# Attention, a gated layer and a merged layer in one kernel: output products ahead of the last pass, three buffers of split weights, a later input split, and a planner that ranks by PSUM tile

## The chip, the cores and the metric

The kernel runs on one core of one Trainium2 chip. The metric is the device time of one execution in microseconds (us); less is better. Five engines work side by side, each through its own queue of instructions in order: TensorE (PE, with its weight loads PEld), VectorE (DVE), ScalarE (ACT), GpSimd (POOL), and SyncE (SP), which here issues nearly all DMAs.

## The reference

```python
# attention: batch 4, 8 heads, 576 tokens, head_dim 64
scores = scale * np.matmul(q, k.transpose(0, 1, 3, 2))
thresh = np.max(scores, axis=-1, keepdims=True) - tau
scores = np.where(scores >= thresh, scores, -1000000000.0)
scores = scores - np.max(scores, axis=-1, keepdims=True)
attn = np.exp(scores)
attn = attn / (np.sum(attn, axis=-1, keepdims=True) + 1e-09)
attn_out = np.matmul(attn, v)
...
x = attn_out.transpose(0, 2, 1, 3).reshape(2304, 512)
# first layer, 512 -> 1536 -> 512
gate = 1.0 / (1.0 + np.exp(-(x @ w_gate)))
x = gate * (x @ w_val) @ w_out
# second layer, 512 -> 1024 -> 1024 -> 512
return ((x @ w1) * (x @ w2) @ w3) @ w_out2
```

All inputs are fp32, some handed over as float64 and cast on the core.

## The kernel before, in words

Every large product is made of three: each fp32 operand is split into a high part (an ACT copy, line 822) and a low part (a subtraction, line 823, on POOL or DVE), and the function `three` multiplies high by low, low by high and high by high into one PSUM tile. All matmuls carry line 439, that of the helper `mm`.

The program has two halves. In the first, a loop over 144 score blocks (`g`) does the attention: scores `ps_s` on PE, their maximum on DVE (`e`, line 687), two ACT passes over the exponentials (lines 695, 696), a split into two 16-bit halves (`h`, lines 703 and 707), a DMA transpose (`pt`) and the products with the values (`u`). Beside it runs a generator as filler: first `merge_gen`, which multiplies w3 by w_out2 into merged weights kept in DRAM as `sc_m`, then `l1_gen`, the first layer. That layer has four passes over the tokens, three of 512 columns and a last one of two halves of 384. A pass takes 12 units of `ps_h` products (`h_unit`: gate weights `gh`, `gl`, value weights `vh`, `vl`, input `xh`, `xl`), and after each three units an output stage `o_stage`: 4 tiles of `ps_o`, 9 products each. A stage stands in the list `pend` and is issued one unit later. The input of a pass is split by `xsplit(b)`, once the attention of that batch is finished; the last pass waits for all of it. `XR` is the buffer that holds attention output, then the layer's output.

What is issued up to the end of the attention is ordered by the class `Plan`: it builds the dependences, places the instructions forward in time by a table of costs (`order`), then backward (`backward`), and gives each instruction a rank by its backward start; the next forward placing prefers low ranks. Of `ROUNDS` such placings it pins the one whose PE ends first. Kinds of product on PE are told apart by a letter: W are 128-row split products (`ps_h`, `ps_o`).

The second half, after the attention, is ordered by the framework's scheduler from the order of the program. It finishes the last pass, then takes the tokens in three groups of 768. Per group, `x2split` makes seven pairs of input parts `o0h`, `o0l` to `o6h`, `o6l`; `pair` makes 8 feature blocks of products `ps_ab` with weight tiles `wc` (ten buffers, loaded by SP) and splits their results into `abh`, `abl`. Then comes the y stage: `part(i, t)` multiplies block `i` by the merged weights `wm(i)` for six row tiles `t`, 18 products of `ps_y` per `i`. `wm_load(i)` loads `wms` from `sc_m` and splits it:

```python
        for i in range(NF2 - 2):
            for t in range(GT // P):
                part(i, t)
            wms.append(wm_load(i + 2))
```

Of the kernel before, what the change touches and what calls it, by code (L numbers as in the profile page):

```python
# [9 lines left out]
F32R = mybir.dt.float32r  # L10
# [11 lines left out]
class Plan:  # L22
# [12 lines left out]
    STAY = 0  # L35
    NEAR = ("HH", "RH", "TH", "HT", "RT", "TT")
    TURN = {"HW": 86, "RW": 199, "WR": 90, "HR": 90, "TR": 90, "RH": 100, "RT": 145, "TW": 5, "HT": 34}
    ROUNDS = 6

    def __init__(self, insts, cut, over, beads=()):  # L40
        self.later = [i for i in insts[cut:] if i.opcode in self.OPS]
# [280 lines left out]
    def backward(self):  # L322
        N, E = len(self.x), ("PE", "DVE", "ACT", "POOL", "SP")
        pred = [self.hard[n] | self.soft[n] for n in range(N)]
        out = [0] * N
        for n in range(N):
            for q in pred[n]:
                out[q] += 1
        lat = [d - s for s, d in zip(self.start, self.done)]
        held = [  # L330
            c[0] if e in ("PE", "SP") else max(60, c[0] - self.OVER[e])
            for c, e in zip(self.cost, self.e)
        ]
        ready, begin = [0.0] * N, [0.0] * N
        avail = {e: [n for n in range(N) if not out[n] and self.e[n] == e] for e in E}
        free = dict.fromkeys(E, 0.0)
        for _ in range(N):
            best = None
            for e in E:
                if not avail[e]:  # L340
                    continue
                n = min(avail[e], key=lambda n: (
                    max(ready[n] + lat[n] - held[n] - free[e] - 1, 0), -self.done[n]
                ))
                s = max(free[e], ready[n] + lat[n] - held[n])
                if best is None or s < best[0]:
                    best = s, e, n
            s, e, n = best
            avail[e].remove(n)
            begin[n] = free[e] = s + held[n]  # L350
            for q in pred[n]:
                out[q] -= 1
                if q not in self.hard[n]:
                    r = begin[n] - lat[q]
                elif self.e[q] == self.e[n] != "SP":
                    r = begin[n] - (lat[q] - 5 if e == "PE" else 0)
                else:
                    r = begin[n] + self.LAG[self.e[q]] + self.LEAD[e]
                ready[q] = max(ready[q], r)
                if not out[q]:  # L360
                    avail[self.e[q]].append(q)
        for i, n in enumerate(sorted(range(N), key=lambda n: -begin[n])):
            self.rank[n] = i

    def pin(self, tc):
        best = None
        for i in range(self.ROUNDS):
            seq = self.order()
            end = max(t for t, e in zip(self.done, self.e) if e == "PE")
            if best is None or end < best[0]:  # L370
                best = end, seq, self.start
            if i + 1 < self.ROUNDS:
                self.backward()
        end, seq, self.start = best
        for n in seq["DVE"]:
            if self.cost[n][1]:
                for m in seq["POOL"]:
                    if self.start[m] > self.start[n]:
                        tc.add_manual_dep(
                            self.x[m], self.x[n].name,  # L380
                            mybir.DependencyInfo(mybir.DependencyClass.Sync, mybir.DependencyReason.DATA),
                            reason="port",
                        )
                        break
        for l in seq.values():
            self.turns(tc, [self.x[n] for n in l])
# [12 lines left out]
def kernel(  # L399
# [23 lines left out]
    P = 128  # L423
    B, H, S, D = q.shape
    NPAIR = H // 2
    NT, DM = out.shape
# [3 lines left out]
    NF = DFF // P  # L430
# [403 lines left out]
    def flush(keep):  # L834
        while len(defer) > keep:
            defer.pop(0)()
# [96 lines left out]
    def open_lx():  # L933
        nonlocal lx
        lx = lx_ctx.enter_context(tc.tile_pool(name="lx", bufs=1))

    def l1_gen():
        w32, whl, gv, pend, raws = {}, {}, {}, [], {}
# [63 lines left out]
        def xsplit(b):  # L1002
            o, k, w = passes[b]
            xh, xl = (lx.tile([P, KC, k * w], F32R, tag=z, name=z) for z in ("xh", "xl"))
            for j in range(k):
                js = slice(j * w, (j + 1) * w)
                for c in range(KC):
                    split(
                        xh[:, c, js], xl[:, c, js], XA[:, c, o + j * w:o + (j + 1) * w],
                        nc.vector if c % 2 else nc.gpsimd,  # L1010
                    )
            return xh, xl
# [80 lines left out]
        for F in range(NFT):  # L1093
            b, f = divmod(F, NF)
            if f == 0:
                while not ready(b):
                    yield None
                if b == B - 1:
                    lx_ctx.close()
                    open_lx()  # L1100
                xhl = xsplit(b)
            k, w = passes[b][1:]
            gv[F] = [
                tuple(
                    (lx if j else lb).tile([P, w], F32R, tag=g, name=g, bufs=4)
                    for g in ("gvh", "gvl")
                )
                for j in range(k)
            ]
            for j in range(k):  # L1110
                yield from h_unit(F, xhl, j)
            whl.pop(("g", F)), whl.pop(("v", F))
            if pend:
                yield from o_stage(*pend.pop())
            if f % SG == SG - 1:
                pend.append((b, f // SG))
                if F == NFT - 1:
                    flush(0)
                    yield from o_stage(*pend.pop())
                    flush(0)  # L1120
# [3 lines left out]
    def ready(b):  # L1124
        return xdone[0] > b and (b < B - 1 or tail[0])
# [145 lines left out]
    NG = NT // GT  # L1271
# [59 lines left out]
    def x2split(g):  # L1331

        t = {m: xp.tile([P, KH, HT], F32, tag="x" + m, name="x" + m) for m in ("1", "2")}
        ops = [
            tuple(xp.tile([P, KH, HT], F32R, tag=f"o{m}{z}", name=f"o{m}{z}") for z in "hl")
            for m in range(7)
        ]
        k1, k2 = slice(0, KH), slice(KH, KC)

        def put(m, x):  # L1340
            split(ops[m][0], ops[m][1], x)

        l, r = (XA[:, :, g * GT + h * HT:g * GT + (h + 1) * HT] for h in range(2))
        put(0, l[:, k1])
        nc.vector.tensor_tensor(t["1"], r[:, k1], l[:, k1], op=ALU.subtract)
        put(1, l[:, k2])
        put(2, t["1"])
        nc.vector.tensor_tensor(t["2"], r[:, k2], t["1"], op=ALU.subtract)
        put(3, t["2"])
        put(4, r[:, k2])  # L1350
        nc.gpsimd.tensor_tensor(t["1"], r[:, k2], r[:, k1], op=ALU.subtract)
        put(5, t["1"])
        nc.gpsimd.tensor_tensor(t["1"], l[:, k2], t["2"], op=ALU.subtract)
        put(6, t["1"])
        return ops

    wg_ = w12_gen()
    x2 = None
    while x2 is None or l1 is not None:
        l1 = run(l1, 4200.0)  # L1360
        if next(wg_, "end") == "end" and x2 is None:
            wctx.close()
            xp = ctx.enter_context(tc.tile_pool(name="xp", bufs=1, side="right"))
            x2 = x2split(0)
# [3 lines left out]
    sp = ctx.enter_context(tc.tile_pool(name="sp", bufs=1))  # L1368
# [90 lines left out]
            at, c0, left = at + m, c0 + m, left - m  # L1459

    def wm_load(i):
        t = sp.tile([P, 2, DM], F32R, tag="wm", name="wm", bufs=2)
        x = sp.tile([P, DM], F32, tag="y", name="wms", bufs=4)
        nc.sync.dma_start(x, sc_m[i])
        split(t[:, 0], t[:, 1], x, nc.gpsimd if i % 2 else nc.vector)
        return t
# [3 lines left out]
    for g in range(NG):  # L1470
        abs_ = [
            tuple(sp.tile([P, GT], F32R, tag=f"ab{z}{f}", name=f"ab{z}{f}") for z in "hl")
            for f in range(NF2)
        ]
        for i in range(NPR):
            if i == NPR - 1:
                wms = [wm_load(0), wm_load(1)]
            pair(x2, i, abs_)
        if g + 1 < NG:
            x2 = x2split(g + 1)  # L1480
        pss = [bank("ps_y") for _ in range(GT // P)]
        def part(i, t):
            h, l = abs_[i]
            ts_ = slice(t * P, (t + 1) * P)
            three(
                pss[t], (h[:, ts_], l[:, ts_]), (wms[i][:, 0], wms[i][:, 1]), i == 0, i == NF2 - 1
            )

        for i in range(NF2 - 2):
            for t in range(GT // P):  # L1490
                part(i, t)
            wms.append(wm_load(i + 2))
        end = len(nc.cur_bb.bb.instructions)
        for t in range(GT // P):
            part(NF2 - 2, t)
            part(NF2 - 1, t)
            out_rows(g, t, pss[t])
# [36 lines left out]
```

## Time and profile before

| what | us |
|---|---|
| median of 3 runs (1042.97 to 1045.5) | 1044.69 |
| profiled execution, its own time | 1041.44 |
| its span, first to last instruction | 1039.5 |
| PE busy / DVE / ACT / POOL | 985.5 / 616.7 / 652.9 / 699.3 |

The profile is of one execution. Its span leaves out 1.9 us around the first and the last instruction. Starts of rows are counted from the span's start. Matmuls are pipelined: a row's length is from issue to the modelled end, so the distance of two starts tells what a product costs PE, not its length.

### The profile page before, as it was taken

How to read it: one execution, taken by the hardware profiler on the slowest of the kernel's cores; microseconds unless marked ns; L12 is line 12 of the kernel's file. 1: busy time of each engine (PE TensorE's matmuls, PEld its weight loads, DVE VectorE, ACT ScalarE, POOL GpSimd, SP SyncE). 2: the span in 40 equal slices, each digit the busy share in tenths (PEclk: the TensorE clock that was granted, in tenths of full speed). 3: DMA queues.
4: the chain of work that ended last, by engine and by line, in shares of the span. 5: the costliest groups of instructions: out<-in, count | busy, mean ns of one | idle time of the engine just before them, and what ended most of it. 6: DMA issues, size and time to landing. Idle time of an engine off the chain costs nothing.

```text
span 1039.5 us, 20101 instructions
## 1 busy us (share of the span) xinstructions
PE 985.5 (95%) x7152; PEld 834.5 (80%) x7152; DVE 616.7 (59%) x1158; ACT 652.9 (63%) x1327; POOL 699.3 (67%) x595
## 2 busy tenths in 40 slices
PE   3699978999999999999999989999999999999997
PEld 2456546777777778777877889999999989989996
DVE  7877856676765444465443367767766716743741
ACT  5888978998899878799788545545422422422221
POOL 4865877999989976878887657758654804642530
PEclk9999989999999999999999999999999999999999
DMA  8999999999999986769865656665668529826922
GB/s 234 241 216 250 249 255 232 247 244 265 236 249 221 229 164 150 161 141 205 178 137 135 135 180 226 233 223 193 222 228 256 167 91 323 247 79 195 311 71 61
DMA packets 295444, 210.01 MB, mean 202 GB/s; under 512 B 220592, under 2 KB 249264, under 8 KB 295344
## 3 DMA queue, kind: packets, MB, share of 16 engines
q1 hardware_dynamic: 294944, 208.07, 77.8%
q8 instruction: 57, 0.93, 0.4%
q10 hardware_dynamic: 400, 0.66, 0.2%
q14 instruction: 43, 0.35, 0.1%
HBM read 133.17 MB, written 30.93 MB: 158 GB/s over the span
## 4 chain that ended last, share of the span: by engine, by line
PE 71%; ACT 7%; issue 6%; POOL 5%; DVE 5%; DMA 5%; SPq 1%; POOLq 0%; DVEq 0%; ACTq 0%
PE ps_h L439 25%; PE ps_ab L439 15%; PE ps_o L439 12%; PE ps_y L439 6%; PE ps_s L439 6%; PE u L439 3%; ACT ps_s L695 2%; ACT e L696 2%; DMA XR<-in_moe_w_out_dram 2%; PE ps L439 2%; POOL h L707 1%; DMA XR<-in_moe_w_dram 1%; DVE e L687 1%; DMA XR<-in_moe_w_val_dram 1%; ACT h L703 1%
## 5 line engine op out<-in xcount | busy, mean ns | idle before, releaser
L707 POOL TENSOR_TENSOR h<-e,h 128x576 f16<-128x576 f32 x144 | 184.5, 1289 | 70.8 <-ACT h L703 39.7
L687 DVE TENSOR_SCALAR_CACHE_REDUCE e<-ps_s,tauc 128x576 f32<-128x576 f32 x144 | 114.8, 813 | 77.5 <-PE ps_s L439 22.8
L695 ACT ACTIVATE ps_s<-ps_s,nt 128x576 f32<-128x576 f32 x144 | 101.7, 711 | 48.4 <-DVE e L687 47.8
L696 ACT ACTIVATE e<-ps_s,ebias 128x576 f32<-128x576 f32 x144 | 106.7, 743 | 4.0
L703 ACT ACTIVATE h<-e 128x576 f16<-128x576 f32 x144 | 97.5, 686 | 1.6 <-DMA pt<-h 1.0
L439 PE MATMUL ps_h<-xl,gh 128*128 128x512 f32 (+1 forms) x240 | 92.1, 384 | 2.5 <-POOL xl L823 2.5
L439 PE MATMUL ps_y<-wm,abh 128*128 128x512 f32 x288 | 91.7, 391 | 1.7 <-POOL wm L823 1.4
L439 PE MATMUL ps_h<-xl,vh 128*128 128x512 f32 (+1 forms) x240 | 91.5, 381 | 1.7 <-DVE yk L593 1.2
L439 PE MATMUL ps_o<-gvl,oh 128*128 128x512 f32 (+1 forms) x240 | 90.1, 376 | 1.5 <-DVE XR L1070 1.5
L439 PE MATMUL ps_o<-gvh,ol 128*128 128x512 f32 (+1 forms) x240 | 89.3, 372 | 0.0
L439 PE MATMUL ps_h<-xh,vl 128*128 128x512 f32 (+1 forms) x240 | 89.2, 372 | 0.0
L439 PE MATMUL ps_h<-xh,gl 128*128 128x512 f32 (+1 forms) x240 | 89.1, 371 | 0.0
L439 PE MATMUL ps_h<-xh,gh 128*128 128x512 f32 (+1 forms) x240 | 89.0, 371 | 0.0
L439 PE MATMUL ps_h<-xh,vh 128*128 128x512 f32 (+1 forms) x240 | 89.0, 371 | 0.0
L439 PE MATMUL ps_o<-gvh,oh 128*128 128x512 f32 (+1 forms) x240 | 88.8, 371 | 0.0
L439 PEld LDWEIGHTS <-pt 128*128 128x128 f16 x2240 | 73.5, 99 | 19.1 <-issue 17.0
L823 POOL TENSOR_TENSOR gl<-w,gh 128x512 fp32r<-128x512 f32 x42 | 54.4, 1294 | 25.8 <-ACT gh L822 25.2
L823 POOL TENSOR_TENSOR gvl<-gr,gvh 128x512 fp32r<-128x512 f32 (+1 forms) x48 | 60.2, 1255 | 13.0 <-ACT gvh L822 12.5
L822 ACT ACTIVATE abh<-r 128x384 fp32r<-128x384 f32 x48 | 24.2, 521 | 69.2 <-DVE r L1397 69.1
L439 PEld LDWEIGHTS ps_y<-wm,abh 128*128 128x128 f32 x288 | 54.1, 188 | 13.2 <-POOL wm L823 1.9
L439 PE MATMUL ps<-wo,t 128*128 128x512 f32 x128 | 62.6, 607 | 0.0
L439 PE MATMUL ps_s<-xk,xq 64*128 64x288 f32 x256 | 36.8, 362 | 26.0 <-ACT e L696 23.5
(191 smaller groups left out, 2797.7 us busy)
## 6 DMA issues: line engine op xcount, KB each, us to landing
wc<-sc_c SPq DMA_DIRECT2D x168, 256.0 KB, 3.3
w<-sc_w SPq DMA_DIRECT2D x35, 768.0 KB, 5.0
sc_c<-wc SPq DMA_DIRECT2D x56, 256.0 KB, 2.8
XR<-in_moe_w_out_dram SPq DMA_DIRECT2D x20, 512.0 KB, 5.3
sc_w<-w SPq DMA_DIRECT2D x11, 768.0 KB, 6.6
XR<-in_moe_w_dram SPq DMA_DIRECT2D x16, 512.0 KB, 5.3
raw<-in_moe_w_dram SPq DMA_DIRECT2D x16, 512.0 KB, 4.4
XR<-in_moe_w_gate_dram SPq DMA_DIRECT2D x12, 512.0 KB, 4.8
```

Of the source, the lines that this page charges most:

```text
L439: return nc.tensor.matmul(out_, lhsT, rhs, start=first, stop=last)
L687: nc.vector.tensor_scalar(e, x["ps"], tauc, None, op0=ALU.add, op1=ALU.min, accum_out=nt)
L695: nc.scalar.activation(x["ps"], x["ps"], AF.Prelu, scale=-1.0, bias=x["nt"], alpha=STEEP)
L696: nc.scalar.activation(x["e"], x["ps"], AF.Exp, bias=ebias, accum_out=prep[pr]["sum"][:, s:s + 1])
L703: nc.scalar.activation(x["h16"][:, 0:S], x["e"], AF.Copy)
L707: nc.gpsimd.tensor_tensor(hb[:, S:2 * S], st[g]["e"], hb[:, 0:S], op=ALU.subtract)
L822: nc.scalar.activation(hi, x, AF.Copy)
L823: (lo_eng or nc.gpsimd).tensor_tensor(lo, x, hi.bitcast(F32), op=ALU.subtract)
```

## The change

Four edits. The planner makes ten placings instead of six, and after each backward one it gives all W products that write the same PSUM tile the lowest rank of that tile, so that a tile once begun is preferred until it is full. In `l1_gen`, the last output stage of the third pass is issued before the last pass's first unit, not after it. The split merged weights have three buffers instead of two. The next group's `x2split` is written behind the second part of the y stage, not ahead of the stage.

```diff
-    ROUNDS = 6
+    ROUNDS = 10
...
         for i, n in enumerate(sorted(range(N), key=lambda n: -begin[n])):
             self.rank[n] = i
+        low = {}
+        for n in range(N):
+            if self.form[n] == "W":
+                t = self.io[n][1][0].tensor.name
+                low[t] = min(low.get(t, N), self.rank[n])
+        for n in range(N):
+            if self.form[n] == "W":
+                self.rank[n] = low[self.io[n][1][0].tensor.name] + self.rank[n] * 1e-6
...
                 xhl = xsplit(b)
+            if F == (B - 1) * NF and pend:
+                flush(0)
+                yield from o_stage(*pend.pop())
...
-        t = sp.tile([P, 2, DM], F32R, tag="wm", name="wm", bufs=2)
+        t = sp.tile([P, 2, DM], F32R, tag="wm", name="wm", bufs=3)
...
-        if g + 1 < NG:
-            x2 = x2split(g + 1)
         pss = [bank("ps_y") for _ in range(GT // P)]
...
             wms.append(wm_load(i + 2))
+            if i == 1 and g + 1 < NG:
+                x2 = x2split(g + 1)
```

Lines behind an edit move by up to 11: 439 becomes 447, 822 becomes 830.

What the planner makes of it, on PE in the middle of the attention. The number behind a tile's name tells one buffer from the next. First before the change, around the tile `ps_h_4170`:

```order
L439 MATMUL ps_h_4170<-xl_2327,gh_3933 128x512
L439 MATMUL ps_h_4170<-xh_2326,gl_3934 128x512
L439 MATMUL ps_h_4170<-xh_2326,gh_3933 128x512
L439 MATMUL ps_h_4170<-xl_2327,gh_3933 128x512
L763 MATMUL ps_x_4207<-ident_64,xn_4122 128x128 x4
L439 MATMUL ps_h_4170<-xh_2326,gl_3934 128x512
L439 MATMUL ps_h_4170<-xh_2326,gh_3933 128x512
L439 MATMUL ps_h_4170<-xl_2327,gh_3933 128x512
L439 MATMUL ps_s1_92<-xk_3803,xq_3805 128x288
L439 MATMUL ps_s0_91<-xk_3803,xq_3805 128x288
```

And after it, on PE around the same tile:

```order
L447 MATMUL ps_h_4170<-xh_2326,gl_3934 128x512
L447 MATMUL ps_h_4170<-xh_2326,gh_3933 128x512
L447 MATMUL ps_h_4170<-xl_2327,gh_3933 128x512
L447 MATMUL ps_h_4170<-xh_2326,gl_3934 128x512
L447 MATMUL ps_h_4170<-xh_2326,gh_3933 128x512
L771 MATMUL ps_x_4207<-ident_64,xn_4122 128x128 x4
L447 LDWEIGHTS pt_3953
L447 MATMUL u_4178<-vh_3616,pt_3953 128x64
```

The twelve products of the tile were cut by four transposes and by a group of scores; now they stand together, and transposes and value products follow.

The end of the attention on PE: the last transposes (`xt`, `xn`) and what follows, before the change:

```order
L767 MATMUL ps_s0_91<-ident_64,xt_8801 128x128
L763 MATMUL ps_x_8804<-ident_64,xn_8800 128x128 x4
L439 MATMUL ps_h_8907<-xl_8886,gh_8679 128x384
L439 MATMUL ps_h_8907<-xh_8885,gl_8680 128x384
L439 MATMUL ps_h_8907<-xh_8885,gh_8679 128x384
L439 MATMUL ps_h_8907<-xl_8886,gh_8679 128x384
```

After it:

```order
L447 MATMUL ps_o_8913<-gvl_8567,oh_8625 128x512
L447 MATMUL ps_o_8913<-gvh_8566,ol_8626 128x512
L447 MATMUL ps_o_8913<-gvh_8566,oh_8625 128x512
L775 MATMUL ps_s0_91<-ident_64,xt_8801 128x128
L771 MATMUL ps_x_8804<-ident_64,xn_8800 128x128 x4
L447 MATMUL ps_o_8903<-gvl_8658,oh_8705 128x512
L447 MATMUL ps_o_8903<-gvh_8657,ol_8706 128x512
L447 MATMUL ps_o_8903<-gvh_8657,oh_8705 128x512
L447 MATMUL ps_o_8913<-gvl_8658,oh_8705 128x512
```

Of the 36 moved `ps_o` products 12 stand ahead of the transposes and 24 behind them; the last pass's `ps_h` follows these.

ACT at the start of the first group's y stage, before the change (`wm_11581` is the third of the eight `wm`, `wm_11604` the fourth):

```order
L822 ACTIVATE o5h_11535<-x1_11523 128x768
L822 ACTIVATE abh6_10797<-r_11463 128x384
L822 ACTIVATE abh7_10799<-r_11493 128x384
L822 ACTIVATE abh7_10799<-r_11519 128x384
L822 ACTIVATE wm_11581<-wms_11582 128x512
L822 ACTIVATE o6h_11537<-x1_11523 128x768
L822 ACTIVATE wm_11604<-wms_11605 128x512
```

After it (`wm_11570` is the fourth; the third, `wm_11547`, stands some forty rows earlier, right behind the second):

```order
L830 ACTIVATE o5h_11587<-x1_11575 128x768
L830 ACTIVATE abh6_10797<-r_11463 128x384
L830 ACTIVATE abh7_10799<-r_11493 128x384
L830 ACTIVATE abh7_10799<-r_11519 128x384
L830 ACTIVATE wm_11570<-wms_11571 128x512
L830 ACTIVATE o6h_11589<-x1_11575 128x768
L830 ACTIVATE wm_11627<-wms_11628 128x512
```

The place behind the last `abh` now belongs to a `wm` that is wanted one part later.

## Rows read from the trace of the kernel before

**Rows 1.** The page: span, engines, POOL's busy tenths and PE's clock in 40 slices.

```profile
span 1039.5 us, 20101 instructions
PE 985.5 (95%) x7152; PEld 834.5 (80%) x7152; DVE 616.7 (59%) x1158; ACT 652.9 (63%) x1327; POOL 699.3 (67%) x595
...
POOL 4865877999989976878887657758654804642530
PEclk9999989999999999999999999999999999999999
```

**Rows 2.** Two stretches: length, then busy us of PE, PEld, DVE, ACT, POOL.

```profile
208.00:260.00 52.00, 50.08 (x405) 39.31 (x403) 36.01 (x73) 46.84 (x95) 50.04 (x43) 1.00 1.07 255
...
312.00:364.00 52.00, 52.00 (x429) 41.43 (x426) 27.52 (x62) 46.80 (x98) 48.59 (x41) 1.00 1.07 225
```

**Rows 3.** All waits of PE after 600 us: total, times, longest.

```profile
PE ps_h L439 <- POOL xl L823: 2.5, 1, 2.5
PE ps_y L439 <- POOL wm L823: 1.4, 1, 1.4
PE ps_y L439 <- DVE wm L823: 0.3, 1, 0.3
```

**Rows 4.** Timeline at the attention's end: start, length, instruction, idle time before it.

```profile
597.84 0.33 PE L767 MATMUL ps_s<-ident,xt 128*128 128x128 f32 x1 [0.18 <-DVE xt L753]
598.44 0.66 PE L763 MATMUL ps_x<-ident,xn 128*128 128x128 f32 x4 [0.27 <-DVE xn L748]
601.55 0.45 PE L439 MATMUL ps_h<-xl,gh 128*128 128x384 f32 x1 [2.45 <-POOL xl L823]
...
599.13 0.69 ACT L774 ACTIVATE XR<-ps_x,vi 128x512 f32<-128x512 f32 x1 [0.30 <-PE ps_x L763]
599.90 3.42 ACT L822 ACTIVATE xh<-XR 128x384 fp32r<-128x384 f32 x8
...
600.50 4.86 POOL L823 TENSOR_TENSOR xl<-XR,xh 128x384 fp32r<-128x384 f32 x4 [2.01 <-ACT xh L822]
```

**Rows 5.** The chain that ended last: an output stage and one part.

```profile
610.14 8.20 PE ps_o L439 x36
...
924.18 4.09 PE ps_y L439 x18
```

**Rows 6.** Timeline of the y stages of the second and the last group.

```profile
908.93 0.39 PE L439 MATMUL ps_y<-wm,abh 128*128 128x512 f32 x1
...
917.83 0.61 ACT L822 ACTIVATE wm<-wms 128x512 fp32r<-128x512 f32 x1
...
1025.20 0.63 ACT L822 ACTIVATE wm<-wms 128x512 fp32r<-128x512 f32 x1 [3.50 <-PE ps_y L439]
...
1025.91 1.26 POOL L823 TENSOR_TENSOR wm<-wms,wm 128x512 fp32r<-128x512 f32 x1 [6.87 <-ACT wm L822]
...
1027.23 0.51 PE L439 MATMUL ps_y<-wm,abh 128*128 128x512 f32 x1 [1.43 <-POOL wm L823]
```

**Rows 7.** Timeline of PE at three passages between kinds of product.

```profile
569.08 0.39 PE L439 MATMUL ps_h<-xh,vh 128*128 128x512 f32 x1
569.39 0.54 PE L439 MATMUL ps_s<-xk,xq 64*128 64x288 f32 x4
...
570.38 0.50 PE L439 MATMUL ps_h<-xl,vh 128*128 128x512 f32 x1
570.72 0.40 PE L439 MATMUL ps_h<-xh,vl 128*128 128x512 f32 x1
...
572.70 0.48 PE L439 MATMUL ps_o<-gvl,oh 128*128 128x512 f32 x1
573.02 0.40 PE L439 MATMUL ps_o<-gvh,ol 128*128 128x512 f32 x1
```

**Rows 8.** Timeline of PE: two waiting score groups between merging and first pass.

```profile
152.74 0.85 PE L439 MATMUL ps_s<-xk,xq 64*128 64x288 f32 x4 [4.75 <-ACT e L696]
160.77 0.53 PE L439 MATMUL ps_s<-xk,xq 64*128 64x288 f32 x4 [2.22 <-ACT e L696]
```

## The prediction

> **What bounds the kernel now.** I read the page first: TensorE (PE) works for 985.5 of 1039.5 us, and no other engine passes 67% [rows 1]. So the question at each place is whether PE waits, and for whom. The stretches say where. From 312 us on PE is busy all the time, 52.00 of 52.00 [rows 2]; before that it is not, and there GpSimd (POOL) is nearly full, 50.04 of 52 us in 208 to 260 [rows 2], nines in the page's slices from 182 us on [rows 1]. The waits of PE after 600 us are three kinds only, 4.2 us in all: once for `xl`, the low part of the last pass's input, and twice for `wm`, the split merged weights [rows 3]. Two conclusions follow. What lets a wait go after 312 us saves just that wait, and there are few. And since PE is full, work that merely changes place saves nothing; only waits filled and cheaper passages from one kind of product to another count.
>
> **Part 1: output products of the third pass ahead of the last pass.** The place is 597 to 602 us [rows 4]. PE transposes `xt` at 597.84 and `xn` at 598.44. Transposes follow each other at (0.66 - 0.33) / 3 = 0.11 us, so 0.60 - 0.11 = 0.49 us are lost between these two, and the fourth of `xn` is through at 598.44 + 4 x 0.11 = 598.88. The next product starts at 601.55: another 2.67 us. In between runs a chain: ScalarE (ACT) copies to `XR` (0.69), splits off `xh` (from 599.90), POOL subtracts `xl` (from 600.50), PE starts. The change puts 36 products here, 12 ahead of the transposes and 24 behind (second order fence). They cost 8.20 us wherever they stand [rows 5], 0.228 each: 2.7 us ahead, which covers the wait for `xn`, and 5.5 us behind, against a chain of 2.67. So 0.49 + 2.67 = **3.2 us** go, with 2.8 us to spare. What else moves with them: four evacuations on VectorE (DVE), no DMA. If PSUM banks for the moved products came free late, the gain would shrink towards 0; the upper bound is the 3.2 itself. I take 3.2, since the banks of the attention are given back here.
>
> **Part 2: three buffers of `wm`, input split later.** With two buffers the split of `wm(i+2)` waits until `part(i)` is through. In the last group that shows nakedly: ACT splits at 1025.20, POOL from 1025.91 for 1.26 us, PE starts at 1027.23 after a wait of 1.43 us [rows 6]. In the first two groups the order hides most of it: PE runs products of the next group's pairs in the gaps, and only 0.3 us of waiting is left [rows 3]. So the third buffer, which on paper takes away six waits per group, can only win 1.4 + 0.3 = 1.7 us, and 0.1 us for each product that restarts the row (0.51 long against 0.39): **1.9 us**. The bound below is 0: the new order has no filler any more (144 products of `ps_y` in a row, but for two of `ps_ab`), so a late split would now be a bare wait. The split that could be late is the fourth one. It now stands where the third stood on ACT, behind the last `abh` (third order fence), at 917.83 in the second group, 8.9 us after that stage's first product at 908.93 [rows 6]. A part takes 4.09 us [rows 5], so the fourth is wanted 12.3 us after 908.93, at 921.2; split and subtraction (0.61 + 1.3 us) end about 919.8, if POOL takes it at once. 1.4 us to spare, so I keep the 1.9. The later input split (seven copies on ACT, eleven operations on DVE and POOL, no DMA) adds nothing: in the new order of ACT its `o` copies stand where they stood. `wms` loads: one more goes early on SP's queue; the eighth still waits there for a buffer freed by the fourth's split, with rows of output and later `wc` loads behind it, whose ten buffers are filled ahead. No cost.
>
> **Part 3: ranks by PSUM tile, ten rounds.** This re-plans everything up to the end of the attention, and the time must be read from what PE's order becomes. Passages between kinds of product have a price [rows 7], against 0.228 for a 512-column product: from such a product to a score 569.08 to 569.39, 0.31, so 0.08 more; from a score back, the first product 570.38 to 570.72, 0.34, so 0.11 more; back from attention's value products 572.70 to 573.02, 0.32, so 0.09 more. Counted over the two orders, from the 480th score product on, where PE is full: passages to scores 29 then 25, from scores 21 then 8, from value products 44 then 35: 4 x 0.08 + 13 x 0.11 + 9 x 0.09 = 2.6 us less. Between the 270th and the 480th: 16 then 11, 7 then 4, 20 then 15: 0.4 + 0.3 + 0.45 = 1.2 us, nearly all PE time too. Together **3.8 us**. (First fence: the twelve products of one tile were cut twice, now they stand together.)
>
> The early part has more in it. Before 312 us PE waits for ACT's exponentials; around the change from merging to the first pass by 4.75 us at 152.74 and 2.22 us at 160.77 [rows 8]. Before, the first products of `ps_h` stood behind the second of these score groups; now 36 of them stand ahead of it, right behind the `xn` transposes. They can fill the 2.22 us. Bounds: 0 if their inputs are as late as the scores' were, 6.97 if the whole stretch moves up. I take **2.0**, the nearer wait.
>
> In this stretch the granted clock of TensorE was also lower: the sixth slice of the page, 130 to 156 us, shows 8 tenths where all the others show 9 or more [rows 1], so part of it ran at 1.2 instead of 2.4 GHz, beside these waits of PE. The Trainium skill, TensorE: Matmul & The Clock Gate, section "What's actually happening", says that the lower level is the default and that activity releases it. By that rule filling the waits would also keep the clock up, and the sum would be nearer its upper bound; by the row alone, whose low stretch lies with the first wait, which no moved product fills, nothing is added. I add nothing.
>
> **Sum.** 3.2 + 1.9 + 3.8 + 2.0 = 10.9 us off the profiled execution's 1041.44: 1030.5. The median of the three runs is 1044.69, 3.25 above that execution, so the forecast is 1044.69 - 10.9 = **1033.8 us**. A difference of 0.3% (3.1 us) is about the least that this measurement tells from none.
>
> **Rivals.**
> B, the new plan wins nothing: passages get cheaper, but scores now wait behind whole tiles of 9 or 12 products (up to 2.7 us), and ACT, DVE and POOL return the gain as later waits of PE. For it: before, a tile was cut just to let scores in. Against: PE never waited after 312 us, so there is slack. Left are parts 1 and 2, 5.1 us: 1039.6.
> C, the early stretch is filled in full: 4.75 + 2.22 instead of 2.0, 5.0 us more: 1028.8. For it: ACT and PE both stand idle there. Against: the first wait has no new product ahead of it.
> D, the plan sets the attention back: 36 products ahead of the score group at 160.77 hold it for 8.2 us if their inputs come as late as before; behind it POOL, at 50.04 of 52 us, can't make up more than 2 us in each such stretch. Then POOL is the bound, PE's cheaper passages don't count, and 8.2 - 5.1 = 3.1 or more are lost: 1047.8. It decides if that score group starts more than some 5 us later than 160.77.
> E, small losses in the plan (2 us) and the fourth `wm` late in two groups (1.4 us each) leave nearly nothing: 1044.4.
>
> **How the numbers follow.** Forecast 0.55 (own range 1029 to 1038), B 0.22, C 0.12, E 0.06, D 0.05. Faster by over 0.3% are the forecast, C and nearly all of B: 0.86; within 0.3% E and 0.03 of B: 0.09; slower D: 0.05. The range 1027 to 1042 leaves out D, E and the far end of C.
>
> **What would show it.** Part 1: no wait for `xl`; from the `xn` transposes to the last pass's first product only the 24 moved products, 5.5 us. Part 2: no wait of PE for `wm`, `ps_y` in one row of 32.7 us, and in the second group no gap ahead of the fourth part. Part 3: fewer "issue" gaps of PE's weight loads; the end of the attention about 5 us earlier; the score group of 160.77 no later than 163. The forecast is wrong if PE shows waits again between 312 and 600 us, or if POOL's nines, which end at 364 us, go on beyond.

## The result and the profile after

The changed kernel takes 1030.24 us (median of 5 runs, 1028.08 to 1031.81), the kernel before 1044.69 (5 runs, 1040.44 to 1045.5). The ratio is 0.9869, with a 95% interval of 0.9843 to 0.9895: 13.7 us less (11.0 to 16.4). The profiled execution of the changed kernel took 1028.8 us. All line numbers of helpers move down by 8 (439 is now 447, 823 is 831).

The page of the changed kernel, against [rows 1]:

```profile
span 1027.0 us, 20097 instructions
...
PE 982.6 (96%) x7152; PEld 838.1 (82%) x7152; DVE 614.9 (60%) x1158; ACT 656.3 (64%) x1327; POOL 700.9 (68%) x595
...
POOL 4866888899998977778887667758644805553431
PEclk9999999899999999999999999999999999999999
```

In this pair of profiles PE is busy for 2.9 us less in a span that is 12.5 us shorter, so most of the gain is idle time of PE. In a second pair (`e12_before` and `e13_after`, below) it is 6.5 of 11.1 us, so one pair does not settle the shares. The slice with an 8 in the clock is still there, two slices later. POOL's nines now end at 359 us, with an 8 among them; before, they ended at 364.

The chain that ended last, of the changed kernel (start us, us, what), against [rows 5] and, for the place, [rows 4]:

```profile
590.90 0.26 PE u L447 x9
591.16 2.82 PE ps_o L447 x12
593.98 0.11 PE ps_s L775
594.09 0.44 PE ps_x L771 x4
594.52 5.49 PE ps_o L447 x24
600.02 33.30 PE ps_h L447 x192
...
749.80 58.27 PE ps_ab L447 x336
...
898.96 12.25 PE ps_y L447 x54
911.21 0.35 PE ps_ab L447 x2
911.56 20.46 PE ps_y L447 x90
...
989.91 32.65 PE ps_y L447 x144
1022.57 0.02 issue
```

From 590.90 on the chain is PE alone. Before, it left PE here and ran through DVE, ACT and POOL. The three engines' work is still done, but now beside the 24 moved products. The trace has no wait of PE at all from 600 us on, where [rows 3] had three, and only 0.2 us between 312 and 600 us.

Where the 12.5 us came from, by landmarks of the two chains. The attention's last value products end at 597.41 before and at 591.16 now: 6.25 us. From there to the first `ps_ab` it was 162.4 us (to 759.81) and is 158.6: 3.8 us. From there to PE's end it was 275.3 (to 1035.06) and is 272.8: 2.5 us.

The waits of PE up to 600 us, first of the kernel before, then of the changed one (us in total, times, longest):

```profile
PE ps_s L439 <- ACT e L696: 23.9, 11, 5.0
```

```profile
PE ps_s L447 <- ACT e L704: 11.6, 7, 5.0
PE u L447 <- DMA pt<-h: 7.8, 3, 5.2
...
PE ps_h L447 <- DVE yk L601: 2.7, 1, 2.7
```

Scores wait 12.3 us less for the exponentials. New waits took most of that back: value products for a DMA transpose (7.8 us, before 0.4) and one `ps_h` product for `yk` (2.7, before 1.2).

### The profile page after: what moved, and what is told of

The parts are those of the page before. It is cut to its first block, busy times and chain, and to the rows that moved or that the text cites. A ratio compares the mean times of both kernels' runs of the same rounds, so it can differ in the third digit from the quotient of the medians.

```text
span 1027.0 us, 20097 instructions
## 1 busy us (share of the span) xinstructions
PE 982.6 (96%) x7152; PEld 838.1 (82%) x7152; DVE 614.9 (60%) x1158; ACT 656.3 (64%) x1327; POOL 700.9 (68%) x595
## 4 chain that ended last, share of the span: by engine, by line
PE 70%; ACT 2%; DVE 1%; DMA 1%; issue 0%; POOL 0%; POOLq 0%; DVEq 0%; ACTq 0%
PE ps_h L447 22%; PE ps_ab L447 17%; PE ps_o L447 13%; PE ps_y L447 10%; PE ps_s L447 5%; PE u L447 2%; PE ps_t L546 0%; DMA pt<-h 0%; ACT e L704 0%; PE ps_x L771 0%; ACT ps_s L703 0%; DMA vnat<-in_v_dram 0%; DVE e L695 0%; DVE gr L1048 0%; DVE vm L607 0%
## 5 line engine op out<-in xcount | busy, mean ns | idle before, releaser
L447 PE MATMUL ps_y<-wm,abh 128*128 128x512 f32 x288 | 89.4, 389 | 0.0
L1048 DVE SCALAR_TENSOR_TENSOR gr<-th,ps_h 128x512 f32<-128x512 f32 (+1 forms) x60 | 37.9, 631 | 57.3 <-PE ps_h L447 38.2
L447 PE MATMUL u<-vh,pt 128*128 128x64 f16 x640 | 56.2, 195 | 7.8 <-DMA pt<-h 7.8
L447 PEld LDWEIGHTS ps_y<-wm,abh 128*128 128x128 f32 x288 | 54.1, 188 | 11.1
L831 POOL TENSOR_TENSOR abl<-r,abh 128x384 fp32r<-128x384 f32 x24 | 24.7, 1030 | 55.5 <-ACT abh L830 53.5
```

The lines of the kernel that those rows point to most:

```text
L447: return nc.tensor.matmul(out_, lhsT, rhs, start=first, stop=last)
L831: (lo_eng or nc.gpsimd).tensor_tensor(lo, x, hi.bitcast(F32), op=ALU.subtract)
L1048: nc.vector.scalar_tensor_tensor(r, t, 1.0, pss["v"][:, 0:w], op0=ALU.add, op1=ALU.mult)
```

## The experiments

**Each edit alone.** Built without the ranks, ten rounds give exactly the order of before on all five engines, and so does the later input split alone; beside a third `wm` buffer it changes no order either. The further rounds and the later input split therefore have no effect of their own. The other three parts were run alone, each on the kernel before.

The planner's part (`e1_plan`) and, with six rounds in place of ten, `e7_ranks6`:

```diff
-    ROUNDS = 6
+    ROUNDS = 10
...
+        low = {}
...
+                self.rank[n] = low[self.io[n][1][0].tensor.name] + self.rank[n] * 1e-6
```

> The kernel before with the planner's edit alone (ranks by PSUM tile, ten rounds). Theory, the three parts add up and the attention's end moves as it did in the changed kernel: last transpose of the attention near 591.5 us instead of 597.8 us, PE's wait for xl (2.5 us) and the three waits for wm still there, 6.3 us less in all: ratio about 0.994. Rival, the earlier end of the attention is eaten at the pass boundary, since the waits there grow when PE arrives earlier: ratio 0.998 to 1.000 and a wait for xl of 5 us or more. Second rival, the plan is the whole gain: ratio 0.988.

> The kernel before with ranks by PSUM tile but six rounds (ten rounds without the ranks give the same order as before on all engines, so this tells what the rounds add to the ranks). Theory, the ranks do it and further rounds are a small choice among like plans: 4 to 7 us less, ratio 0.993 to 0.996. Rival, the gain is the luck of the plan found between the seventh and the tenth round: ratio 0.998 or more.

The moved output stage (`e2_ostage`):

```diff
             if f == 0:
...
                 xhl = xsplit(b)
+            if F == (B - 1) * NF and pend:
+                flush(0)
+                yield from o_stage(*pend.pop())
```

> The kernel before with the output stage moved ahead of the last pass, alone. Theory: the wait for xl goes and no other takes its place, first pair product 3.3 us earlier than 759.8 us: ratio 0.9968, at the edge of what five rounds can tell. Rival, the moved products only hide the wait when the plan has changed too (their own inputs come late otherwise): a wait of PE ahead of ps_o instead, under 1 us gained, ratio 1.000.

The third buffer (`e4_wm3`):

```diff
-        t = sp.tile([P, 2, DM], F32R, tag="wm", name="wm", bufs=2)
+        t = sp.tile([P, 2, DM], F32R, tag="wm", name="wm", bufs=3)
```

> The kernel before with three buffers of split merged weights, alone; the input split stays where it was (written later or not, all five engines get the same order). Theory: the waits for wm go, 2.4 us between the first pair product (759.8 us) and the end of PE: ratio 0.9977. Rival, the third buffer needs the later input split, and PE waits ahead of the fourth part, 1 us or more, in the first two groups: ratio 0.999 to 1.000.

| alone | us, median | ratio to before (95%) | us won |
|---|---|---|---|
| planner, 10 rounds | 1037.01 | 0.9947 (0.9928 to 0.9967) | 5.5 (3.4 to 7.5) |
| planner, 6 rounds | 1036.38 | 0.9937 (0.9920 to 0.9953) | 6.6 (4.9 to 8.4) |
| output stage | 1038.17 | 0.9950 (0.9931 to 0.9968) | 5.2 (3.3 to 7.2) |
| third buffer | 1039.77 | 0.9977 (0.9959 to 0.9995) | 2.4 (0.5 to 4.3) |

(Microseconds are the ratio's distance from 1 times 1044.69. The ratios are to the kernel before as it was run beside these, with a median of 1041.86 us in 17 runs; the plain differences of medians are 4.9, 5.5, 3.7 and 2.1.) 5.5 + 5.2 + 2.4 = 13.1 against 13.7 for all together: the parts add up, as far as intervals of some 2 us on either side of each can tell. Each takes away its own waits and leaves the others. The waits of PE after 312 us, cut to those of [rows 3], first of the planner's part, then of the output stage alone, then of the third buffer alone:

```profile
PE ps_h L447 <- POOL xl L831: 2.5, 1, 2.5
PE ps_y L447 <- POOL wm L831: 1.4, 1, 1.4
PE ps_y L447 <- DVE wm L831: 0.3, 1, 0.3
```

```profile
PE ps_y L439 <- POOL wm L823: 1.4, 1, 1.4
...
PE ps_y L439 <- DVE wm L823: 0.3, 1, 0.3
```

```profile
PE ps_h L439 <- POOL xl L823: 2.5, 1, 2.5
```

**Which half of the plan wins.** `e8_late` gives ranks by tile only to the W products behind the first 432, those of the second and third pass, and `e9_early` only to the first 432 (`ws[:432]`):

```diff
+        ws = [n for n in range(N) if self.form[n] == "W"]
+        mine = set(ws[432:])
...
+            if n in mine:
```

> The kernel before with ten rounds and ranks by PSUM tile for the tiles of the second and third pass alone; before 270 score products the order stays nearly as it was (no product of the first pass ahead of the waiting score group). From the 480th score product on the passages fall as in the changed kernel (to scores 29 to 24, from scores 21 to 7, from value products 44 to 35: 2.8 us by their prices). Theory, passages have these prices: 2.8 us less, ratio 0.9973, PE's idle time before 312 us unchanged near 45 us. Rival, the plan's gain is all in the early stretch: ratio 1.000.

> The counterpart: ranks by tile for the first pass alone; from the 480th score product on the passages stay (29, 21, 43), before it they fall as in the changed kernel (1.4 us), and 24 products of the first pass stand ahead of the score group that waited at 160.8 us. Theory: 1.4 us of passages and some 3 us of idle time before 312 us (45 to 41 us), 4.3 us less: ratio 0.9959. Rival, the early idle time is given back later, because POOL is full there: ratio 0.9985 to 1.000.

The late half alone takes 1039.19 us, ratio 0.9973 (0.9957 to 0.9988): 2.8 us won (1.3 to 4.5). The early half alone takes 1040.43, ratio 0.9983 (0.9971 to 0.9995): 1.8 us (0.5 to 3.0). The late half agrees with the price of passages that was taken from [rows 7].

One sign of that theory failed: PE's idle time before 312 us was to stay near 45 us and is 40.0, so this plan differs early too. The profiles still tell where its time comes from. PE's last four score products up to the 480th, in the two profiles of the kernel before and in that of the late half (where line 439 is 449):

```profile
310.93 0.43 PE L439 MATMUL ps_s<-yk,xq 64*128 64x288 f32 x4
```

```profile
309.26 0.43 PE L439 MATMUL ps_s<-yk,xq 64*128 64x288 f32 x4
```

```profile
310.61 0.43 PE L449 MATMUL ps_s<-yk,xq 64*128 64x288 f32 x4
```

From there to the attention's last value product (which ends at 597.41, 596.20 and 594.46) PE has the same products left in the three traces but for one, and needs 286.48 and 286.94 us before, 283.85 with the late half: 2.6 and 3.1 us less, where 2.8 were worked out. Up to there the late half gains nothing clear of the scatter: PE idles less, but 12.5 us of its work ran at the lower clock, against 5.5 and 4.8 us before.

The early half wins something, but less than the theory's figure, whose ratio lies outside the interval; the interval reaches into the range of the rival, by which the idle time that was saved is given back later. The idle time before 312 us did fall as the theory said, to 40.6 us.

**The rounds beside the rest.** `e10_six` is the changed kernel with six rounds.

> The changed kernel with six rounds instead of ten. Theory, the rounds add nothing that can be measured: ratio 0.986 to 0.988, as the changed kernel. Rival, ten rounds are worth a microsecond or more: 0.989 or above.

It takes 1029.12 us, ratio 0.9875 (0.9854 to 0.9897), where the changed kernel has 0.9869: ten rounds instead of six add nothing that shows.

**Why the moved stage won more than its wait.** Alone it won 5.2 us, and what the prediction counted at the boundary is 3.2. A second profile of the kernel before (`e12_before`) was to show whether the granted clock falls at that wait.

> The kernel before, profiled once more. In its first profile the granted clock stayed at 1.00 through the wait for xl at 600 us; in all five variants that keep this wait it fell to half for 3.4 us there, and 1.5 us more passed between the last pass's first product and the first pair product (159.6 against 158.1 us). Theory, this is the usual case and the first profile was the exception: a stretch below 0.9 within 5 us of that wait, 159.6 us. Rival, the variants' order brings it: clock 1.00, 158.1 us.

It took 1041.58 us, and the clock did fall. The chains of the first profile of the kernel before, of the second, and of the planner's part alone show the first 48 products behind the same wait:

```profile
601.55 8.60 PE ps_h L439 x48
```

```profile
600.35 9.91 PE ps_h L439 x48
```

```profile
596.98 10.16 PE ps_h L447 x48
```

The windows of 6 us there, of the second profile and of the changed kernel (length, busy us of PE, PEld, DVE, ACT, POOL, granted clock, DMA share, GB/s):

```profile
600.00:606.00 6.00, 5.65 (x25) 5.65 (x26) 4.56 (x4) 3.97 (x9) 4.14 (x4) 0.73 0.78 256
```

```profile
600.00:606.00 6.00, 6.00 (x37) 6.00 (x36) 3.97 (x7) 3.63 (x9) 4.97 (x5) 1.00 0.51 162
```

In the second profile the granted clock is 0.73 in these 6 us, part of them at 1.2 instead of 2.4 GHz, behind PE's wait of 2.46 us for `xl`. The same 48 products take 1.31 us longer than in the first. Of seven profiles that have this wait, six have the slow products (9.91 to 10.19 us), and one, the first of the kernel before, has not (8.60). In the profiles with the stage moved PE is busy through the boundary and the clock stays at 1.00 there. The Trainium skill, TensorE: Matmul & The Clock Gate, section "What's actually happening", says that the lower level is the default and that activity releases it; these rows agree at this place, though not in every execution.

**The changed kernel again, and further along the same way.** `e13_after` repeats the changed kernel. `e11_every` and its repeat `e14_every` put an output stage ahead of every pass, and `e15_r24` lets the planner try 24 rounds.

```diff
-            if F == (B - 1) * NF and pend:
+            if f == 0 and pend:
```

> The changed kernel with the last output stage of every pass issued ahead of the next pass, not only of the last one. Theory, PE has no waits at the inner boundaries (planned order, next to no idle time from 312 to 600 us), so nothing more is won: ratio 0.986 to 0.988. Rival, the planner starts from a better order: 0.985 or less.

> The changed kernel again, beside the next one. Both theories: ratio 0.986 to 0.988; no fall of the clock between 590 and 612 us.

> The kernel of e11 again (output stage ahead of every pass), on the same chip as the changed kernel. Theory, its 1.5 to 2 us against the changed kernel are the plan's: attention's last value product 1.5 us earlier again, ratio 0.0015 below that of e13. Rival, they are the spread of runs: ratios within 0.0007 of each other.

> The changed kernel with 24 rounds. Its order has the price of passages of the changed one (2.8 against 2.7 us before, 5.8 against 6.0 us after the 480th score product). Theory, further rounds choose among like plans: ratio within 0.001 of e13. Rival, more rounds keep paying: 0.002 lower or more.

The repeat takes 1029.11 us, ratio 0.9859 (0.9830 to 0.9888). A stage ahead of every pass takes 1027.39, ratio 0.9859 (0.9839 to 0.9879), and the second time 1027.64, ratio 0.9850 (0.9827 to 0.9874). With 24 rounds it is 1027.17, ratio 0.9842 (0.9814 to 0.9870). Both beat the kernel before. Against the changed kernel, run beside `e14_every` and `e15_r24`, they are 1.5 and 1.9 us ahead, and all intervals overlap: a hint, not a result. In ratios that is 0.0009 and 0.0017 lower, between what theory and rival had said in both cases.

How far one profile can be trusted in the early part, the windows from 0 to 312 us tell; two profiles of the kernel before, then two of the changed one (columns as above):

```profile
0.00:312.00 312.00, 267.04 (x2332) 194.05 (x2333) 222.48 (x471) 266.74 (x542) 247.62 (x214) 0.98 1.06 243
```

```profile
0.00:312.00 312.00, 270.01 (x2343) 196.97 (x2344) 223.61 (x476) 267.72 (x546) 249.14 (x215) 0.99 1.06 244
```

```profile
0.00:312.00 312.00, 272.31 (x2379) 199.40 (x2380) 226.41 (x476) 270.95 (x551) 253.65 (x219) 0.98 1.04 247
```

```profile
0.00:312.00 312.00, 269.68 (x2348) 197.49 (x2348) 225.32 (x470) 270.29 (x549) 252.11 (x218) 0.98 1.06 247
```

PE's busy time in this stretch differs by 3.0 us between the two profiles of the kernel before, and by 2.6 between the two of the changed one. The means differ by 2.5 us. The early gain is as large as the scatter of one profile, so a pair cannot size it. Three more profiles help, since PE has the order of before up to the attention's last value product in `e2_ostage` and `e4_wm3` as well, and that of the changed kernel in `e1_plan`. PE's idle time in this stretch is 45.0, 42.0, 46.8 and 43.7 us with the order of before, 39.7, 42.3 and 41.0 with the changed one: 3.4 us less on average.

**All profiles together.** Two distances between landmarks hardly vary from profile to profile, and so size parts 1 and 2 more closely than the times do. From the attention's last value product to the first `ps_ab` it is 162.40 us in the first profile of the kernel before, 163.73 to 164.00 in the six others with the wait for `xl`, and 158.64 or 158.65 in all seven with the stage moved. From there to PE's end it is 275.18 to 275.28 us in the seven profiles with two `wm` buffers and 272.76 or 272.77 in the seven with three. The end of the attention varies more: 597.41, 596.20, 598.73 and 600.58 us with PE's order of before, 591.16, 592.66 and 592.83 with that of the changed kernel, 6.0 us earlier on average.

## Why the prediction was right

The forecast was 1033.8 us with 10.9 us won; it became 1030.24 and 13.7, by the mechanisms that were forecast and inside its own range. The sum was too small all the same: 10.9 lies just below the interval of 11.0 to 16.4. The terms:

| term | forecast | timed alone | by the profiles |
|---|---|---|---|
| Part 1, moved output stage | 3.2 | 5.2 (3.3 to 7.2) | 5.1 to 5.4, in one 3.8 |
| Part 2, third buffer | 1.9 | 2.4 (0.5 to 4.3) | 2.4 to 2.5 |
| Part 3, behind the 480th score product | 2.6 | 2.8 (1.3 to 4.5), late half | 2.6 and 3.1 |
| Part 3, passages from 270 to 480 (1.2) and early waits (2.0) | 3.2 | 1.8 (0.5 to 3.0), early half | about 3, an estimate: 6.0 less the row above |

**Part 1** is the term that was mis-sized. The wait itself went as forecast. The trace has no wait for `xl`, and between the transposes and the last pass's first product there are only 24 `ps_o` products, 5.49 us (5.5 forecast). By the chains, 4.14 us lay before between the last value product (597.41) and the last pass's first product (601.55). Now it is 8.86 (591.16 to 600.02), of which the 36 moved products are 2.82 + 5.49: 0.55 are left, so 3.6 us went against 3.2. The rest is the wait for `xt`, 0.18 us in [rows 4], which the first twelve products also cover and the term did not count, and shorter issue. What the term left out is the clock behind the wait, 1.3 to 1.6 us for the first 48 products in six of seven profiles. The profile of before that the forecast read was the seventh. So the sentence that a wait which goes after 312 us "saves just that wait" is the step that fell short. The times alone don't show it, since their interval begins at 3.3; the landmarks do: 3.8 us where the clock held, 5.1 to 5.4 where it fell. The rule of the clock was weighed in the prediction at another place, the early stretch, and there adding nothing was right, since the clock did not get better (Part 3, early).

**Part 2** went as worked out, down to the margin, and won half a microsecond more. The timeline of ACT and POOL in the second group of the changed kernel, for the fourth `wm`:

```profile
907.70 0.62 ACT L830 ACTIVATE wm<-wms 128x512 fp32r<-128x512 f32 x1
908.84 1.30 POOL L831 TENSOR_TENSOR wm<-wms,wm 128x512 fp32r<-128x512 f32 x1
```

ACT splits 8.74 us after the stage's start at 898.96 (8.9 forecast), POOL is through at 910.14, and the fourth part is wanted when the first 54 products end, at 911.21. 1.1 us are to spare, where 1.4 were forecast; POOL took it 0.5 us late, the "if" of that step. The two `ps_ab` products stand just there, but they cover no wait. The row of `ps_y` in the last group is 32.65 us (32.7 forecast). By the landmarks the part won 2.4 to 2.5 us, not 1.9. Before, products of `ps_ab` broke the rows of `ps_y` in the first two groups twelve times, now once; the term priced two such breaks. That the others make up the rest was not measured. That the later input split costs nothing holds, since it moves nothing.

**Part 3, late.** Passages at the prices of [rows 7] were the right account: 2.6 against 2.8. Gaps of PE's weight loads that end in "issue", from 312 to 590 us, were one thing to look for. Before, then after:

```profile
PEld L439 <- issue: 11.5, 44, 0.3
```

```profile
PEld L447 <- issue: 7.9, 34, 0.3
```

Ten such gaps and 3.6 us fewer, as forecast. PE's products overlap its weight loads, so no price follows from them; the price rests on the late half's time and on the stretch from the 480th score product.

**Part 3, early.** Here the term was too high by the early half's own time, about right by the profiles, and the check that went with it was wrong. The timeline of PE around the change from merging to the first pass, after the change, against [rows 8]:

```profile
151.98 0.24 PE L447 MATMUL u<-vh,pt 128*128 128x64 f16 x1 [5.17 <-DMA pt<-h]
...
157.83 0.51 PE L447 MATMUL ps_h<-xl,gh 128*128 128x512 f32 x1 [0.92 <-POOL xl L831]
...
166.78 0.54 PE L447 MATMUL ps_s<-xk,xq 64*128 64x288 f32 x4
```

The `ps_h` products did come ahead of the second score group, and that group no longer waits. But the first wait became 5.17 us for a transpose instead of 4.75 for the exponentials, 0.92 us for `xl` are new, and the wait for `yk` grew. In the balance the idle time fell by 3.4 us (above), more than the 2.0 that were to be filled. The clock took part of it back. The first products behind the wait for `yk`, in the first profile of the changed kernel, then in the second:

```profile
181.77 0.80 PE L447 MATMUL ps_h<-xl,vh 128*128 128x512 f32 x1 [2.69 <-DVE yk L601]
182.36 0.63 PE L447 MATMUL ps_h<-xh,vl 128*128 128x512 f32 x1
182.79 0.63 PE L447 MATMUL ps_h<-xh,vh 128*128 128x512 f32 x1
```

```profile
185.21 0.50 PE L447 MATMUL ps_h<-xl,vh 128*128 128x512 f32 x1 [2.67 <-DVE yk L601]
185.55 0.40 PE L447 MATMUL ps_h<-xh,vl 128*128 128x512 f32 x1
185.79 0.40 PE L447 MATMUL ps_h<-xh,vh 128*128 128x512 f32 x1
```

In the first they come 0.43 us apart, at the lower clock; in the second 0.24. But there the earlier low stretch lasts longer. The low stretches before 312 us, the kernel before twice, then the changed one's two, then the one of its second profile:

```profile
145.90:156.10 10.20, 5.45 (x56) 4.61 (x57) 5.65 (x12) 7.92 (x17) 7.02 (x7) 0.50 1.00 279
```

```profile
149.30:156.10 6.80, 4.76 (x69) 4.48 (x70) 5.39 (x10) 4.83 (x12) 3.96 (x4) 0.50 1.02 275
```

```profile
150.20:157.10 6.90, 4.92 (x44) 3.77 (x44) 4.44 (x10) 5.15 (x11) 4.78 (x5) 0.51 1.07 319
180.90:187.80 6.90, 6.03 (x16) 4.45 (x18) 2.62 (x5) 5.44 (x13) 6.69 (x7) 0.51 1.02 329
```

```profile
150.00:163.70 13.70, 8.78 (x53) 6.77 (x54) 9.59 (x15) 11.40 (x24) 8.68 (x7) 0.50 1.10 282
```

PE worked at the lower clock for 5.45 and 4.76 us before, for 10.95 and 8.78 us after the change. What each of the two pieces of this term kept apart was not measured.

The score group starts at 166.78, where "no later than 163" had been said, and 6.0 us behind 160.77, past the point from which **rival D** was to decide. The kernel did not become slower. The step of D that fails is that a later score group must set POOL back. The windows of the kernel before from 156 to 208 us, then of the changed kernel from 156 and from 208 us:

```profile
156.00:208.00 52.00, 46.79 (x495) 38.52 (x492) 34.18 (x74) 48.09 (x97) 45.88 (x38) 1.00 1.07 240
```

```profile
156.00:208.00 52.00, 46.97 (x385) 37.05 (x385) 37.87 (x77) 46.08 (x95) 46.96 (x39) 0.92 1.07 266
208.00:260.00 52.00, 51.91 (x470) 42.49 (x469) 34.55 (x70) 48.43 (x97) 51.72 (x44) 1.00 1.02 241
```

POOL does more in both stretches than before (46.96 against 45.88, and 51.72 against 50.04 in [rows 2]), and PE, which had 1.92 us free in the second stretch, is full: 51.91 of 52. So the late score group cost POOL nothing here: what stood ahead of it was PE work that must be done anyway. That the other engines had score blocks in hand meanwhile is the likely reason; it was not measured.

**The other rivals.** B fell, since the planner's part alone wins 5.5 us. C named nearly the right time, 1028.8, with the wrong mechanism: the early part did not win more than forecast. E fell with the fourth `wm` in time.

## What to carry to other kernels

Where one engine is nearly always busy, find its few bare waits and put work under them that must be done anyway; a wait of PE can cost more than its length, because products behind it may run at the lower clock (here 1.3 to 1.6 us more on a wait of 2.46, in six profiles of seven), so take more than one profile before sizing it. Where single profiles scatter, look for a distance between two landmarks that does not: here such distances sized two parts to a few tenths of a microsecond, where the times left 4 open. Work that only changes place still wins where it makes fewer passages between kinds of product, and counting passages in the two orders, at prices from the trace, gave 2.6 us where the time says 2.8 and the profiles 2.6 and 3.1. A late start of one group is no evidence for a loss: ask whether the engine that bounds the stretch has become less busy.

## What the hardware showed that was not expected

With the same program and nearly the same wait, 2.45 and 2.46 us, TensorE's granted clock stayed at 1.00 in one execution and fell to 0.73 over 6 us in another; neither the length of the wait nor its place decides it alone. The wait for `yk` in the changed kernel is a second case: lower clock behind 2.69 us of it in one profile, full clock behind 2.67 in the other. In the early stretch of the changed kernel PE idles less than before, and the clock is worse, not better: 0.94 and 0.92 in 104 to 156 and 156 to 208 us, in the second profile 0.94 and 0.93, where the kernel before had 0.90 and 1.00, then 0.94 and 1.00. What decides where it falls there stays open.
